# A sliding-window attention and maxout FFN kernel: its whole order of work written anew, the last outputs made ordinary units, nine buffers for first-expert results

## The chip, the cores and the metric

The kernel runs on one core of one Trainium2 chip. A core has a matrix engine (TensorE, PE in the profile; its weight loads are PEld), three engines for elementwise work (VectorE or DVE, ScalarE or ACT, GpSimd or POOL) and SyncE (SP), which here only issues DMAs. The engines run side by side, each through its own list of instructions in order, and wait for each other by semaphores. The metric is the time of one execution on the device in microseconds; lower is better.

## The reference

Two stages follow each other. First an attention over 4 batches, 8 heads, 768 positions and 64 dimensions a head, in which a query sees the 96 positions up to its own and the first 8 positions of the sequence, with a bias that falls with the distance. Then an FFN whose hidden layer is the elementwise maximum of three matrix products ("experts").

```python
scores = scale * np.matmul(q, k.transpose(0, 1, 3, 2))
is_global = pos[None, :] < 8
is_local = (rel >= 0) & (rel < 96)
keep = is_global | is_local
dist = np.where(is_global & ~is_local, 96.0, np.abs(rel))
scores = np.where(keep, scores - slopes[:, None, None] * dist, -1e9)
a = softmax(scores)
x = np.matmul(a, v)                      # 3072 tokens x 512
h = np.maximum(np.maximum(x @ w1, x @ w2), x @ w3)   # 512 -> 768
out = h @ w_out                          # 768 -> 512
```

## The kernel before

The 3072 tokens are 24 tiles T of 128, six to a batch; a pair of tiles is a group G. Tile T needs the keys and values of its own tile and of the tile before it (the first tile of a batch of its own alone, so it has half the work); the first 8 keys and values of the batch are copied into the tile's rows once the tile itself is done. The FFN takes the tiles in seven chunks of 4, 2, 2, 4, 4, 4 and 4 tiles (SIZES, line 89): chunk 0 is tiles 0 to 3, chunk 1 tiles 4 and 5, chunk 2 tiles 6 and 7, chunk 3 tiles 8 to 11, and so on to chunk 6, tiles 20 to 23.

There is no loop. The string SCHEDULE (line 24) lists some 780 units, and the last lines of the kernel call one function for each, in that order. A unit puts its instructions at the end of its engine's list, so the string fixes the order of work on every engine; the waits between engines follow from what each instruction reads and writes. A unit is a letter, its arguments with dots between, and after @ the slot of a ring of buffers that it takes. The last argument of many units is the engine: 0 is ACT, 1 DVE, 2 POOL. The units that the text speaks of:

- l (line 223): SP loads part of q, k or v of a group, 512 KB in most cases (first argument 0, 1, 2 for q, k, v; G 12 is a special first load of the first four tiles, in two halves or quarters). c casts it to bf16; v casts values into the rows of tile T.
- x (line 262): PE transposes a group's q and k, and y copies the result from PSUM; X (line 289) does both by a DMA transpose instead.
- b (line 329) puts the bias of a tile into PSUM by matmuls; S (line 338) makes the scores of four heads of tile T, 8 matmuls (4 for the first tile of a batch); e (line 352) is the exponential on ACT; m (line 359) multiplies with a mask on DVE where no bias was put in. B and K make the biases and the masks at the start. G and V copy the first 8 keys and values.
- A (line 380): weights times values, 16 matmuls (8 for the first tile of a batch); n normalises on DVE into xb. t and u transpose a tile of xb by PE and copy it into xT; Z (line 423) does it by DMA.
- w and q load the FFN's weights (staging), W and Q cast them. w123 has three column groups, w0 brings the first and w1 the two others, for expert 0, 1 or 2; q brings w_out.
- F c.f.j (line 428): the first FFN layer for chunk c, column block f of six, expert j: four matmuls of 512 columns (256 for the chunks of two tiles). f (line 441): for expert 0 the result is copied from PSUM to a buffer h01; for expert 1 DVE takes the maximum into it; for expert 2 DVE writes the maximum to ht and h01 is free.
- O c.t (line 465): the second layer for tile t of chunk c, six matmuls of 512 columns into a PSUM bank; o (line 469) copies it to a staging buffer; s (line 473) stores it. D (line 528) are matmuls on zeros into an unused bank.
- E (line 479) makes the outputs of the last chunk with its own lists of banks and buffers: tiles 0 and 1 with the sixth weight held back, tile 2, and tile 3 in parts of 256, 128 and 128 columns, each part copied and stored at once. Behind E stands one more output, `O5.0 o5.0.0 s5.0.2`, of 512 columns, stored in two halves.

PSUM has eight banks; an F or an O takes one, S and A two in a row, and the slot numbers say which. RINGS (line 90) gives the number of buffers of each ring: 7 for loads of q and k (r), 5 for h01, 3 for cast q and k (qb), 4 for transposed q and k (qkT), 4 for xb.

Of the kernel before, what the change touches and what calls it, by code (L numbers as in the profile page):

```python
# [12 lines left out]
FP32 = mybir.dt.float32  # L13
# [16 lines left out]
    w1.1@1 S0.0.0@0 e0.0@3 l2.2.2@2 S2.0.1 v0.0.1 e2.0@4 w0.1@1 v0.1.1 m0.0.1 e2.1@5 v2.1.2 b3.0@4 A1@0  # L30
    V1.1.1 V1.0.2 G2.1 v3.1.2 w0.2@2 A0@2 S3.0.1 e3.0@6 b3.1@6 n1@0 c0.2.2.2@2 S3.1.1 G3.0 A2@0 V2.0.2
    e3.1@7 V2.1.2 n0@1 t0@2 W0.0.2 c1.2.2.1 u0.0@0 x2.1.2@3 y2.1.2.0@2 w1.2@2 x2.0.2@2 A3@4 t1@6 u1.0 n2@2
    y2.0.2.1 t2@7 n3@3 l0.3.2@1 l1.3.2@2 S4.1.0@0 V3.1.2 e4.1@0 V3.0.2 S4.0.0@2 W1.1.2 u2.1 t3@6 G4.1 u3.0
    W2.0.1 S5.1.0@4 e5.1@2 S5.0.0@0 e5.0@1 m4.1.1 W1.0.1 e4.0@3 F0.5.0@7 F0.4.0@6 W2.1.0 F0.3.0@4 f0.3.0.0@0
    F0.2.0@5 f0.4.0.1@1 F0.1.0@6 v4.1.2 v4.0.2 l2.3.2@0 f0.1.0.0@2 q2@0 v5.1.0 F0.0.0@0 F0.5.1@1 F0.4.1@4
    F0.2.1@6 m4.0.1 f0.0.0.0@3 v5.0.0 f0.5.0.0@4 m5.1.1 A4@2 V4.1.0 F0.3.1@0 W0.1.2 f0.4.1.1 W0.2.0 m5.0.1
    f0.5.1.1 F0.0.1@1 F0.1.1@4 V4.0.1 W1.2.0 n4@1 t4@7 A5@2 W2.2.0 c1.3.2.2@0 f0.0.1.1 f0.1.1.1 F0.1.2@1
    n5@0 u4.1@1 f0.1.2.1@0 F0.0.2@4 q0@1 t5@7 u5.0 q1@2 f0.3.1.1 f0.0.2.1 F0.2.2@2 F0.3.2@3 f0.3.2.1
    c0.3.2.0 f0.2.0.0@2 f0.2.1.1 F1.2.0@4 F1.0.2@7 Q2.0 v7.1.2 F1.0.0@5 f1.0.0.1@3 v6.1.2 F1.0.1@3 f0.2.2.1
    f1.0.1.1 f1.2.0.1@0 Q0.2 f1.0.2.1@1 x3.1.2@6 y3.1.2.1@3 F0.4.2@5 f0.4.2.1 l1.4.2@3 v6.0.2 Q1.2 F1.1.0@0  # L40
    F1.2.2@1 l0.4.2@4 l1.6.2@5 F1.2.1@4 f1.2.1.1 F1.3.1@2 f1.2.2.1 F1.3.2@3 v7.0.2 F1.3.0@4 f1.3.0.0@2
    f1.3.1.1 f1.3.2.1 x3.0.2@1 F0.5.2@5 f0.5.2.1 F1.4.0@2 F1.1.1@3 f1.1.0.0@3 y3.0.2.0 S6.0.0@0 S6.1.0@4
    G6.2 c1.4.2.2@1 c0.4.2.2 l0.5.2@0 c0.5.2.2@2 f1.1.1.1 f1.4.0.0@1 e6.0@4 S7.0.0@6 S7.1.0@2 l1.5.2@6
    c1.5.2.2 e6.1@5 c1.6.2.2@0 e7.1@6 F1.4.1@0 e7.0@7 l2.4.2@1 O0.2@1 f1.4.1.1 m7.1.1 x4.1.2@0 F1.5.2@2
# [567 lines left out]
```

## Time and profile before

| | us |
|---|---|
| median of three runs | 176.49 |
| lowest, highest | 175.44, 176.92 |
| span of the profiled execution (first to last instruction) | 174.8 |
| PE busy | 165.9 |
| DVE busy | 131.9 |
| ACT busy | 95.4 |
| POOL busy | 54.7 |
| mean granted TensorE clock | 0.996 |

The profiled execution is one more execution, of which the page gives the span. In the rows, a line such as L433 is a line of the kernel, out<-in names what is written and read, xN counts instructions; "busy, mean ns" is followed by the idle time ahead of them and what ended it. A matmul's listed duration is longer than its pace in a queue, since queued matmuls overlap. The chain of waits names pieces of the path that ended last, with start, length and count. "SPq" rows are SP issuing a DMA; an issue grows longer when the DMA engines are behind.

### The profile page before, as it was taken

How to read it: one execution, taken by the hardware profiler on the slowest of the kernel's cores; microseconds unless marked ns; L12 is line 12 of the kernel's file. 1: busy time of each engine (PE TensorE's matmuls, PEld its weight loads, DVE VectorE, ACT ScalarE, POOL GpSimd, SP SyncE). 2: the span in 40 equal slices, each digit the busy share in tenths (PEclk: the TensorE clock that was granted, in tenths of full speed). 3: DMA queues.
4: the chain of work that ended last, by engine and by line, in shares of the span. 5: the costliest groups of instructions: out<-in, count | busy, mean ns of one | idle time of the engine just before them, and what ended most of it. 6: DMA issues, size and time to landing. Idle time of an engine off the chain costs nothing.

```text
span 174.8 us, 3865 instructions
## 1 busy us (share of the span) xinstructions
PE 165.9 (95%) x1485; PEld 93.6 (54%) x1507; DVE 131.9 (75%) x268; ACT 95.4 (55%) x147; POOL 54.7 (31%) x99
## 2 busy tenths in 40 slices
...
DMA  5999999999899899999996759998990046370035
GB/s 149 352 292 327 402 360 385 270 371 311 229 303 179 139 183 266 267 290 284 165 135 112 114 145 306 305 210 260 231 213 20 0 120 137 121 286 4 0 119 185
DMA packets 66403, 37.36 MB, mean 214 GB/s; under 512 B 24144, under 2 KB 61392, under 8 KB 66384
## 3 DMA queue, kind: packets, MB, share of 16 engines
...
q8 instruction: 12, 0.20, 0.5%
q10 hardware_dynamic: 144, 0.07, 0.1%
q14 instruction: 7, 0.06, 0.1%
...
## 4 chain that ended last, share of the span: by engine, by line
PE 76%; DVE 10%; DMA 6%; ACT 3%; issue 2%; SPq 0%; DVEq 0%
PE psum L433 44%; PE psum L457 17%; PE psum L349 6%; DMA xT<-xb 3%; DMA rawqk<-in_k_dram 3%; DVE P L365 3%; PE psum L391 3%; PE psum L394 2%; PE psum L276 2%; DVE ht L452 1%; DVE xb L403 1%; ACT P L356 1%; PE psum L270 1%; DVE qb L195 1%; PE psum L335 1%
## 5 line engine op out<-in xcount | busy, mean ns | idle before, releaser
L433 PE MATMUL psum<-xT,w 128*128 128x512 bf16 (+1 forms) x491 | 97.5, 348 | 1.5 <-DMA xT<-xb 0.7
L433 PEld LDWEIGHTS <-w 128*128 128x128 bf16 x504 | 47.6, 98 | 42.9 <-DMA xT<-xb 0.9
L356 ACT ACTIVATE P<-psum 128x1024 bf16<-128x1024 f32 (+1 forms) x48 | 43.3, 954 | 10.4 <-PE psum L349 10.3
L449 DVE TENSOR_TENSOR h<-h,psum 128x512 bf16<-128x512 bf16 (+1 forms) x42 | 25.0, 605 | 15.9 <-PE psum L433 12.4
L457 PE MATMUL psum<-wo,ht 128*128 128x512 bf16 (+2 forms) x147 | 33.4, 362 | 0.5
L447 ACT CAST h<-psum 128x512 bf16<-128x512 f32 (+1 forms) x27 | 13.8, 523 | 33.1 <-PE psum L433 29.8
L452 DVE TENSOR_TENSOR ht<-h,psum 128x512 bf16<-128x512 bf16 (+1 forms) x42 | 26.2, 644 | 2.1 <-PE psum L433 0.9
L365 DVE TENSOR_TENSOR P<-P,wmask 128x1024 bf16<-128x1024 bf16 x34 | 25.2, 752 | 2.0 <-ACT P L356 1.7
L457 PEld LDWEIGHTS <-ht 128*128 128x128 bf16 x156 | 13.8, 98 | 13.5 <-DVE ht L452 0.2
L254 POOL CAST va<-rawv 64x512 bf16<-64x512 f32 x28 | 18.5, 668 | 4.8 <-DMA rawv<-in_v_dram 3.7
L323 POOL COPY va<-vaf 4x260 int32<-4x260 int32 x17 | 7.2, 424 | 34.9 <-PE psum L394 34.5
L403 DVE TENSOR_TENSOR xb<-psum,rz 128x512 bf16<-128x512 f32 x24 | 16.6, 692 | 0.8
L201 POOL CAST qb<-rawk 128x512 bf16<-128x512 f32 x12 | 7.5, 654 | 23.7 <-DMA rawk<-in_k_dram 23.7
L349 PE MATMUL psum<-qkT 64*128 64x128 bf16 x352 | 14.4, 217 | 0.5 <-DVE qkT L315 0.4
L391 PEld LDWEIGHTS <-P 128*128 128x128 bf16 x192 | 12.6, 97 | 3.2 <-ACT P L356 0.4
L349 PEld LDWEIGHTS <-qkT 64*128 64x128 bf16 x352 | 10.0, 94 | 7.9 <-issue 5.9
L391 PE MATMUL psum<-va,P 128*128 128x65 bf16 x160 | 12.7, 193 | 0.7 <-DVE ht L452 0.6
L447 DVE CAST h<-psum 128x512 bf16<-128x512 f32 (+1 forms) x15 | 9.1, 615 | 5.1 <-PE psum L433 5.1
L471 ACT COPY staging<-psum 128x512 f32<-128x512 f32 x14 | 8.2, 592 | 8.8 <-PE psum L457 8.8
L201 POOL CAST qb<-rawq 128x512 bf16<-128x512 f32 x14 | 8.9, 664 | 9.0 <-DMA rawq<-in_q_dram 5.0
L394 PEld LDWEIGHTS <-P 128*128 128x128 bf16 x160 | 10.5, 97 | 2.1 <-issue 0.7
L394 PE MATMUL psum<-va,P 128*128 128x65 bf16 x128 | 9.9, 193 | 0.0
...
## 6 DMA issues: line engine op xcount, KB each, us to landing
rawv<-in_v_dram SPq DMA_DIRECT2D x12, 512.0 KB, 7.0
...
rawq<-in_q_dram SPq DMA_DIRECT2D x10, 512.0 KB, 7.1
rawk<-in_k_dram SPq DMA_DIRECT2D x10, 512.0 KB, 7.3
staging<-in_moe_w_dram SPq DMA_DIRECT2D x3, 1024.0 KB, 9.3
staging<-in_moe_w_dram SPq DMA_DIRECT2D x3, 512.0 KB, 8.8
staging<-in_moe_w_out_dram SPq DMA_DIRECT2D x3, 512.0 KB, 6.3
out_dram<-staging SPq DMA_DIRECT2D x5, 128.0 KB, 2.2
```

The source lines that it names most:

```text
L254: copies[how](heads(va(T))[64 * e:64 * e + 64, :, 0:D], src)
L349: nc.tensor.matmul(sp[:, hh, j2, ds], qT(T - ds, 1, hsl, jp), qT(T, 0, hsl, jp), start=not how, stop=True, skip_group_check=True)
L356: nc.scalar.activation(P[:, :, 0:n], sps[T, g].rearrange("p a b d n -> p (a b) d n")[:, :, 0:n], AF.Exp, bias=0.0, scale=scale)
L365: mul(P, P, wmask[:, g, :, 0:2])
L391: nc.tensor.matmul(o, P[:, i, 0], heads(va(T))[:, h], start=True, stop=(t == 0), skip_group_check=True)
L394: nc.tensor.matmul(o, P[:, i, 1], heads(va(T - 1))[:, h], start=False, stop=True, skip_group_check=True)
L403: nc.vector.tensor_tensor(out=x.rearrange("p (g h) d -> p g h d", g=2), in0=o4[:, :, :, 0:64], in1=rz[:, :, :, None].to_broadcast([128, 2, ...
L433: nc.tensor.matmul(ps, w123[f // 2][:, j, dm, (f % 2) * 128:(f % 2) * 128 + 128], xT[c][:, dm], start=(dm == 0), stop=(dm == 3))
L447: copies[how](h01, ps)
L449: nc.vector.tensor_max(h01s[c, f], h01s[c, f], ps)
L452: nc.vector.tensor_max(dst, h01s[c, f].rearrange("p (t e i) -> p t e i", e=2, i=64), ps.rearrange("p (t e i) -> p t e i", e=2, i=64))
L457: nc.tensor.matmul(po, ht[c][:, f, tt * 128:(tt + 1) * 128], wo[:, f, cols], start=(f == 0), stop=(f == NF - 1))
```

## The change

The string is written anew: 802 units for 782, with nearly the same work in another order and with other engines and slots for many of the casts and copies.

- Before F0.4.0, now the first F, stand S0 to S7 (before: S0 to S5 ahead of F0.5.0) and the transposes of group 3. Loads l0.2, l1.2, l1.3 and l0.3 stand ahead of the first weight load w1.0 (before: l0.2 and l1.2), and the weights come in the order w1.0, w0.1, w0.0, l2.2, w0.2, w1.1, w1.2.
- Bias units b: 4 for 7; masks m: 44 for 41. D: 10 matmuls of 512 columns and 18 of 256 in four units (before 10 and 3).
- Tiles 6 and 7 go to xT by DMA (Z) instead of PE (t, u): 17 Z for 15, 7 t for 9.
- Output copies o on DVE: 11 whole ones and one of 128 columns (before 6 and one). Value casts v on POOL: 23 for 32.
- E is gone. O, o and s take optional ranges of weights (f0 to f1) and of columns in steps of 64 (c0 to c1). The last chunk's tiles are ordinary units between the last tiles of chunk 5; tile 6.3 comes in three parts: columns 384 to 511 early, then, last of all, 0 to 255 and 256 to 383. s0.1, s0.3 and s3.3 are stored among them.
- RINGS: h01 9 for 5; r 6 for 7, qb 2 for 3, qkT 3 for 4, xb 3 for 4, rz 3 for 4.

```diff
-RINGS = {'r': 7, 'rv': 3, 'qb': 3, 'qkT': 4, 'sp': 2, 'h': 8, 'P': 8, 'xb': 4, 'xT': 3, 'wst0': 3, 'wst1': 3, 'ht': 2, 'h01': 5, 'rz': 4, 'os': 12}
+RINGS = {'r': 6, 'rv': 3, 'qb': 2, 'qkT': 3, 'sp': 2, 'h': 8, 'P': 8, 'xb': 3, 'xT': 3, 'wst0': 3, 'wst1': 3, 'ht': 2, 'h01': 9, 'rz': 3, 'os': 12}
...
+    def u_O(slot, c, tt, f0=0, f1=NF, c0=0, c1=8):
+        if slot is not None:
+            pos[c, tt, c0] = ring("h", slot, [128, (c1 - c0) * 64], FP32, "po")
+        for f in range(f0, f1):
+            nc.tensor.matmul(pos[c, tt, c0], ht[c][:, f, tt * 128:(tt + 1) * 128], wo[:, f, c0 * 64:c1 * 64],
+                             start=(f == 0), stop=(f == NF - 1))
...
+    def u_o(slot, c, tt, *rest):
+        c0, c1 = rest[:-1] or (0, 8)
+        osts[c, tt, c0] = ring("os", slot, [128, DM], FP32, "ost")[:, 0:(c1 - c0) * 64]
+        copies[rest[-1]](osts[c, tt, c0], pos[c, tt, c0])
...
+    def u_s(slot, c, tt, c0=0, c1=8, queue=0):
+        (nc.sync, nc.scalar)[queue].dma_start(out=out[T * 128:(T + 1) * 128, c0 * 64:c1 * 64], in_=osts[c, tt, c0])
```

The new order where the text speaks of it: the start up to the first F units, the start of chunk 3, and the end.

```text
l0.12.1@0 l1.12.1@1 D10.512@0 l0.12.2@2 R B2.0 B6.0 l0.12.3@3 l1.12.3@4 B4.0 B7.1 K6 c1.12.1.1@0 B0.1 K5 K7 K0
B5.0 c0.12.1.2@1 x12.0.1@0 y1.0.1.1@0 l1.12.2@5 y0.0.1.0@1 K1 K4 K3 l2.0.2@0 D2.256@1 x12.1.1@1 B3.1 y0.1.1.1
...
S6.1.0@0 e6.1@7 u2.1 u3.1 W2.0.2 F0.4.0@6 W0.1.1 F0.0.1@7 F0.1.1@4 v5.1.2 F0.1.0@5 W0.2.0 f0.1.0.0@0 V3.1.1
...
F2.0.1@2 f2.0.1.1 F2.2.0@3 f2.4.0.1@1 c0.7.2.2@1 X13@1 Z8@1 F2.3.2@7 f2.2.0.0@4 X12 l1.7.2@4 c1.7.2.2 Z10 Z9
...
o5.1.1@6 s5.1 s0.3 O6.2@4 s0.1 o6.3.6.8.0@1 s6.3.6.8 o6.2.1@2 s6.2 s3.3 O6.0.0.5.0.8@5 O6.0.5.6.0.8 o6.0.1@10
s6.0 O5.2@4 o5.2.1@6 s5.2 O6.1.0.5.0.8@5 O6.1.5.6.0.8 o6.1.1@1 s6.1 O5.0@4 o5.0.0@3 s5.0 O6.3.0.6.0.4@5
o6.3.0.4.0@10 s6.3.0.4 O6.3.0.6.4.6@6 o6.3.4.6.1@2 s6.3.4.6
```

168 lines of the change are left out of this document (61 added, 107 removed).

## The prediction

> **What bounds the kernel now.** I read the page's head and shares first, then busy time by stretch, the groups by shape, the waits of TensorE, and last the timeline of the start and the end.
>
> ```profile
> span 174.8 us, 3865 instructions
> PE 165.9 (95%) x1485; PEld 93.6 (54%) x1507; DVE 131.9 (75%) x268; ACT 95.4 (55%) x147; POOL 54.7 (31%) x99
> ...
> DMA  5999999999899899999996759998990046370035
> ```
>
> TensorE (PE) is busy for 95% of the span. The DMA line is at 9 until about 85 us, so in the first half the DMA engines are full too. The next fence cuts the span at the first and the last matmul of the first layer of the FFN and at the last matmul of all: window, its length, busy us of PE, PEld, DVE, ACT, POOL, clock, DMA share, GB/s.
>
> ```profile
> 1.19:21.58 20.39, 18.88 (x235) 11.15 (x236) 18.06 (x51) 17.50 (x31) 8.56 (x17) 1.00 1.07 321
> 21.58:171.17 149.59, 146.98 (x1250) 82.43 (x1271) 113.55 (x215) 76.90 (x116) 45.57 (x77) 1.00 0.83 203
> 171.17:174.80 3.63, 0.00 (x0) 0.00 (x0) 0.00 (x0) 0.58 (x1) 0.00 (x0) 0.81 0.43 144
> ```
>
> So the time is a sum of four terms: start 21.58 (until unit F0.5.0), PE work behind it 146.98, PE idle in that stretch 149.59 - 146.98 = 2.61, and a tail of 3.63 behind the last matmul: 174.80. A new order can't remove the work; it can win only in the other three terms, 2.61 + 3.63 and what the start wastes. The page lists no time for the profiled execution beside its span; the median of the runs is 176.49, 1.69 above it, and I carry these 1.69 over.
>
> **The change, term by term.** First the work. The rows give the pace of queued matmuls:
>
> ```profile
> 58.27 2.18 PE psum L433 x20
> 60.45 0.55 PE psum L349 x16
> 155.42 9.23 PE psum L433 x42
> 54.95 0.45 PE psum L418 x8
> ```
>
> A 512-column matmul is paced at 9.23/42 = 0.22 us, one of 256 columns (the x20) at 0.11, a score unit S (8 matmuls) at 0.275, a transpose at 0.056. Counted in the two orders: bias units b go from 7 to 4 (14 matmuls to 8: -4 x 0.22 - 2 x 0.11 = -1.1), PE transposes t from 9 to 7 (-8 x 0.056 = -0.45), warm-up matmuls D from 10 + 3 to 10 + 18 narrow ones (+15 x 0.11 = +1.65). The b and the D all lie ahead of F0, where PE waits anyway (20.39 - 18.88 = 1.5 idle, and the D are filler), so they count nothing by themselves; if they ran late they'd cost at most their 1.65. The six matmuls of the last output tile are still 512 columns in all (before 256 + 128 + 128, after 128 + 256 + 128), and splitting the sums of two other tiles at 5 of 6 weights adds none. Ahead of F0 the new order also does S6 and S7 (2 x 0.14 + 2 x 0.275 = 0.83; tile 6 has one block) and the transposes x3 (16 x 0.056 = 0.90). Work behind F0: 146.98 - 0.83 - 0.90 - 0.45 (t6, t7) = **144.8**.
>
> **The start** is where the new order pays. Here are the exponentials, the first weight's cast and the loads:
>
> ```profile
> 6.34 2.65 SPq L236 DMA_DIRECT2D rawq<-in_q_dram  x1
> 9.11 1.90 SPq L236 DMA_DIRECT2D rawk<-in_k_dram  x1
> 11.05 3.52 SPq L514 DMA_DIRECT2D staging<-in_moe_w_dram  x3
> ...
> 9.06 1.02 ACT L356 ACTIVATE P<-psum 128x1024 bf16<-128x1024 f32 x1 [0.30 <-PE psum L349]
> 11.32 3.54 ACT L356 ACTIVATE P<-psum 128x1024 bf16<-128x1024 f32 x4
> 21.75 1.67 POOL L201 CAST w<-staging 128x512 bf16<-128x512 f32 x2 [3.20 <-DMA staging<-in_moe_w_dram]
> ...
> L201 POOL CAST qb<-rawq 128x512 bf16<-128x512 f32 x14 | 8.9, 664 | 9.0 <-DMA rawq<-in_q_dram 5.0 <-DVE va L325 4.0
> L195 DVE CAST qbq<-rawqq 128x1024 bf16<-128x1024 f32 x1 | 0.7, 694 | 0.1
> ...
> staging<-in_moe_w_dram SPq DMA_DIRECT2D x3, 1024.0 KB, 9.3
> staging<-in_moe_w_dram SPq DMA_DIRECT2D x3, 512.0 KB, 8.8
> ...
> DMA to landing us min/median/max: 7.9/9.2/11.3
> ```
>
> F0.4.0 needs the weight w1.0. Before, four loads of 512 KB stood between the quarter loads and it; now six do (l1.3.2, l0.3.2 moved ahead). At the stretch's 321 GB/s two loads of 0.524 MB are 3.3 us, so w1.0 is issued near 11.05 + 3.3 = 14.3 and lands 9.3 later, at 23.6. Its cast W2.0 moves from DVE to POOL, where a pair of halves takes 1.67 by the row above (1.2 is the best pair): F0 at 24.8 to 25.3. The other chain is ACT: from e1.1 to e6.0, which frees the banks for S6.1 just ahead of F0, it has ten wide exponentials at about 0.95 (three of the 3.54 above and the short one), three short ones at 0.55, and 2.6 of copies: 13.75. From 9.06 that ends at 22.8; the first query cast also moves to POOL (0.66 a half against 0.69 for the whole on DVE) and K1, K4, K3 go ahead of y1.1.1, so e1.1 is rather at 9.6: 23.4, and t3, u3 behind n3 bring it to about 24.3. I take **24.8**: the weight is the later chain. Bounds: 14.3 + 7.9 + 1.2 = 23.4 and 14.3 + 11.3 + 1.7 = 27.3. The following weights (w0.1, w0.0, w0.2, w1.1, w1.2) come at 1.6 us per 512 KB, each about as PE wants it (0.88 per F unit, eight units until w0.2), so they have no cover left; I count 0.2.
>
> **Idle behind F0.** Three waits of before:
>
> ```profile
> PEld L433 <- DMA xT<-xb: 0.9, 1, 0.9
> PE psum L433 <- DMA xT<-xb: 0.7, 1, 0.7
> PE psum L391 <- DVE ht L452: 0.6, 1, 0.6
> ...
> 110.80:111.58 0.78, 0.61 (x16) 0.43 (x14) 0.25 (x1) 0.00 (x0) 0.00 (x0) 1.00 1.15 315
> ...
> L447 ACT CAST h<-psum 128x256 bf16<-128x256 f32 x8 | 2.9, 375 | 5.0 <-PE psum L433 5.0
> L195 ACT CAST qb<-rawq 128x1024 bf16<-128x1024 f32 x2 | 2.1, 1046 | 0.1
> ...
> L424 SPq DMA_TRANSPOSE xT<-xb x15: 1188/1487/2670, 63.0 to 145.2; - x15
> DMA to landing us min/median/max: 2.4/3.4/7.0
> ```
>
> The 0.7 is chunk 3 waiting for its DMA-transposed tiles at 72.8; the 0.6 is A12 waiting for DVE at 83.1; A13 at 111 costs 0.78 - 0.61 = 0.17. The rest of 2.61 (1.2) is spread thin; I keep it. Chunk 3 again: X13 goes out only behind c1.6.2.0 on ACT (0.38 for f2.3.0, 0.22 and 0.59 for the small copy and the output copy between, 1.05 for the cast: 2.2 after F2.3.0), then Z8, X12, l1.7.2, Z10 and Z9 leave SP one after another (four at 1.49, one load 0.58), so Z9 starts 8.8 after F2.3.0 and lands 3.4 later, at 12.2. PE's work in that stretch, summed as above (14 F units of two tiles, two A, one t, three O at 1.3, five S), is 12.4. Wait 0 to 1.4; I take 0.4. Chunk 2 now comes by Z6, Z7 instead of t6, t7: they lie behind X10, which needs c0.5.2.0 behind e8.1; landing about 11 us after S8 against 11.5 of PE work: 0.2. Chunks 4, 5, 6 have 7.1, 5.5 and 5.3 us of PE work between the last A and the first F against about 1.6 of normalising plus 3.4: nothing, though 5.0 of landing would cost 1. Idle: 1.2 + 0.2 + 0.4 + 0.2 = **2.0**, between 1.2 and 4.
>
> DVE carries more, POOL less:
>
> ```profile
> L365 DVE TENSOR_TENSOR P<-P,wmask 128x1024 bf16<-128x1024 bf16 x34 | 25.2, 752 | 2.0 <-ACT P L356 1.7
> L471 DVE COPY staging<-psum 128x512 f32<-128x512 f32 x6 | 4.1, 684 | 0.2 <-PE psum L457 0.2
> L283 DVE COPY qkT<-psum 128x512 bf16<-128x512 bf16 x4 | 2.6, 685 | 0.0
> L254 POOL CAST va<-rawv 64x512 bf16<-64x512 f32 x28 | 18.5, 668 | 4.8 <-DMA rawv<-in_v_dram 3.7
> ```
>
> Three more masks (2.3), five more output copies (3.4), four more y copies (2.7), with the smaller moves +7 us, to 139; POOL loses nine value casts (-6). PE's 165 still covers DVE. The nine h01 buffers let first-expert results leave PSUM early and cost nothing; the smaller rings (r, qb, qkT, xb, rz one less each) delay loads, the tightest being X20, still about 2 us ahead of S20.
>
> **The tail.**
>
> ```profile
> 171.19 0.58 ACT L471 COPY staging<-psum 128x512 f32<-128x512 f32 x1 [1.03 <-PE psum L457]
> 171.80 0.81 SPq L477 DMA_DIRECT2D out_dram<-staging  x2
> ...
> L462 DVE COPY staging<-psum 128x128 f32<-128x128 f32 x1 | 0.3, 291 | 3.1 <-PE psum L457 3.1
> L462 ACT COPY staging<-psum 128x256 f32<-128x256 f32 x1 | 0.4, 372 | 0.1
> ...
> out_dram<-staging SPq DMA_DIRECT2D x5, 128.0 KB, 2.2
> out_dram<-staging SPq DMA_DIRECT2D x1, 64.0 KB, 2.1
> ```
>
> Before: copy 0.58, second issue near 172.2, landing 2.2, 0.4 to the end. After: the 256-column copy ends 0.06 after the last matmul, its issue takes 0.41, then the last 64 KB go: 0.48 + 2.1 + 0.4 = **3.0**, 0.6 less. It would be 3.6 if the outputs saved up for the end (s0.1, s0.3, s3.3) fill the queue.
> [...]
>
> **Sum:** 24.8 + 144.8 + 2.0 + 3.0 = 174.6, against 174.8; with 1.69, **176.3 us**, no change. The start gives away 3.2 and has 1.7 of it back as work done early; t, idle and tail bring 0.45, 0.6 and 0.6.
>
> **Rivals.** *The weights come early and the new order's slack is real.* Start 23.4, idle 1.2: 23.4 + 144.8 + 1.2 + 3.0 = 172.4, time 174.1. For it: before, DVE's cast of w1.0 found it there without a listed wait. Against: POOL waited 3.2 us for w0.0.
> *The weights come late* (the other side): w1.0 at the row's 11.3, start 27.3, and each weight behind it late as well, idle 3.2: 27.3 + 144.8 + 3.2 + 3.0 = 178.3, time 180.0. It decides once the start passes 27, or 26 with over 2.8 of idle.
> *DVE becomes the bound* between F0 and F1, where, counted unit by unit with the rows' durations, it has 11.8 against 11.1 on PE: +0.7 there and as much at chunk 2, 176.0, time 177.7. Against: a worse ratio before chunk 3 of the old order (16.4 on 14.5, counted alike) cost 0.7.
> *It doesn't do what it says:* the tail stays 3.6: 175.2, time 176.9.
> *The array goes cold while it waits for weights.* The first ten matmuls pace 0.43 instead of 0.22:
>
> ```profile
> 1.19 4.45 PE L532 MATMUL psum<-zeros 128*128 128x512 bf16 x10 [1.19 <-DVE cap L550]
> ```
>
> If PE idles long enough ahead of F0, eight F units at that pace cost 8 x 4 x 0.21 = 6.7 more, time 183.0; the widest gap by the bounds is 27.3 - 24.3 = 3.0.
> [...]
>
> **How the numbers follow.** Forecast 0.40, early weights 0.31, late weights 0.19, DVE 0.06, tail 0.03, cold 0.01. About 1% is what a measurement of this kernel tells from no change: faster is under 174.7, slower over 178.3. Faster 0.31, within 1% 0.49, slower 0.20. The range reaches from a little below the early case to short of the late one, 173.4 to 179.2; the forecast's own is 174.8 to 178.2.
>
> **What would show it.** First L433 matmul near 24.8 with a wait of PE or POOL on the weight's DMA; PE busy behind it near 144.8; a wait on xT near F3 under 1.4 and none by DVE at A12 and A13; the last matmul to the end 3.0. The prediction is wrong if F0 starts before 23.4 or after 27.3, or if idle behind F0 exceeds 4.

## The result, and the profile after

The changed kernel takes **184.15 us** (median; 182.88 to 185.23) against 176.27 for the kernel before beside it (175.44 to 176.92): a ratio of 1.0449, interval 1.0388 to 1.0510. The forecast was 176.3, with a range up to 179.2. The change is slower, by 7.9 us. The profile below is of the longest of its four executions, 185.23 us.

The head of the page after, with the shares of PE and the DMA line:

```profile
span 183.5 us, 3876 instructions
PE 168.8 (92%) x1487; PEld 94.9 (52%) x1508; DVE 138.1 (75%) x274; ACT 96.5 (53%) x149; POOL 50.9 (28%) x91
PEclk9999969999999999999999999999999999999999
DMA  4999999999917899999998999998903870030294
```

Two things are new: a 6 in the line of the granted clock, in the slice from 22.9 to 27.5 us, and a 1 in the DMA line, in the slice from 50.5 to 55 us, where the line of before has 9. Now the same three stretches as in the prediction: until the first F, from there to the last matmul, and the tail.

```profile
1.19:28.17 26.98, 22.46 (x285) 14.37 (x286) 19.98 (x53) 21.08 (x35) 15.66 (x27) 0.94 1.08 306
28.17:179.31 151.14, 146.37 (x1203) 80.54 (x1224) 117.51 (x218) 74.88 (x115) 34.69 (x59) 1.00 0.79 191
179.31:183.50 4.19, 0.00 (x0) 0.00 (x0) 0.29 (x1) 0.07 (x1) 0.00 (x0) 0.91 0.38 129
```

| term, us | before | forecast | after | after less forecast |
|---|---|---|---|---|
| start | 21.58 | 24.8 | 28.17 | +3.4 |
| PE busy behind F0 | 146.98 | 144.8 | 146.37 | +1.6 |
| idle behind F0 | 2.61 | 2.0 | 4.77 | +2.8 |
| tail | 3.63 | 3.0 | 4.19 | +1.2 |
| sum | 174.8 | 174.6 | 183.5 | +8.9 |

All four terms miss to the same side. The sum misses by 8.9 and the median by 7.9, since this execution lies 1.1 above the median. Busy and idle have to be read together, as 1487 of 1508 matmul records are there, and 1485 of 1507 in the profile before. Together they are 151.14 against 146.8, +4.3. Two runs of experiment 10 kept every record. On the kernel before with the new tail, the stretch of 148.90 holds 148.27 busy and 0.63 idle. In the kernel after with three stores moved, which changes nothing in PE's list, the stretch is:

```profile
28.01:179.88 151.87, 147.82 (x1227) 80.57 (x1224) 117.74 (x218) 74.84 (x115) 34.68 (x59) 1.00 0.78 190
```

That is 4.05 idle. So most of the 2.61 of idle before was records that are missing, and the change adds about 3.4 us of idle behind F0.

**The start.** The timeline of PE and of POOL there (it lists the first F from 28.10 on):

```profile
21.09 0.19 PE L384 MATMUL psum<-va,P 128*128 128x65 bf16 x1 [1.60 <-POOL va L247]
26.84 0.73 PE L342 MATMUL psum<-qkT 64*128 64x128 bf16 x20 [0.34 <-DVE qkT L280]
28.10 1.25 PE L426 MATMUL psum<-xT,w 128*128 128x512 bf16 x4
...
14.71 1.92 POOL L194 CAST qb<-rawk 128x512 bf16<-128x512 f32 x2
16.58 1.17 POOL L194 CAST qb<-rawq 128x512 bf16<-128x512 f32 x2
18.30 2.74 POOL L247 CAST va<-rawv 64x512 bf16<-64x512 f32 x2
24.73 1.17 POOL L194 CAST w<-staging 128x512 bf16<-128x512 f32 x2
```

A2 stands 1.60 us for the values of tile 2. Their cast v2.1.2 is the second of the pair at 18.30, behind v3.1.2 and the casts c1.2 and c0.2. The weight that the forecast called the late chain is cast from 24.73 to 25.9, and the first F comes 2.2 later. In between, the clock falls. The trace records half clock from 22.30 to 25.72; these are that stretch and the 3.41 us ahead of it:

```profile
18.89:22.30 3.41, 1.69 (x39) 1.46 (x39) 2.17 (x6) 2.12 (x5) 2.31 (x4) 1.00 1.07 361
22.30:25.72 3.42, 3.42 (x47) 2.74 (x45) 2.69 (x5) 2.31 (x3) 3.30 (x6) 0.50 1.10 347
```

**Chunk 3.** SP stands at X10 from 46.2 to 54.24, and behind X10 on SP stand Z6, Z7 and all later loads and transposes. The totals of waits, a window of the time in which SP stands, and PE from F3 on:

```profile
SPq L285 <- ACT qb L188: 7.0, 2, 3.6
...
PEld L426 <- DMA xT<-xb: 1.4, 1, 1.4
...
52.00:54.00 2.00, 2.00 (x20) 1.25 (x19) 1.27 (x3) 2.00 (x3) 1.31 (x3) 1.00 0.01 4
...
79.01 5.34 PE L426 MATMUL psum<-xT,w 128*128 128x512 bf16 x23 [0.98 <-DMA xT<-xb]
84.87 0.19 PE L387 MATMUL psum<-vaf,P 128*128 128x65 bf16 x1 [0.48 <-POOL vaf L247]
92.92 0.20 PE L384 MATMUL psum<-va,P 128*128 128x65 bf16 x1 [0.60 <-DVE P L358]
95.18 4.48 PE L426 MATMUL psum<-xT,w 128*128 128x512 bf16 x19 [0.49 <-DVE ht L445]
```

Almost no transfer runs from 52 to 54 (share 0.01). The two waits of X on ACT, 7.0 together, are X10's for c0.5.2.0 (3.4) and X13's for c1.6.2.0 (3.6). Ahead of its 3.4, X10 stands for another 4.6 us for PE: it takes over the buffer of tiles 6 and 7, which the scores S8 still read. In that time the loads issued earlier still fill the DMA engines (share 1.09 from 48 to 50). The ring has a third buffer, which nothing uses until X18; no run gave it to X10. F3 starts at 79.0, against 72.8 before, and has idled 0.98 for its transposed tiles; the weight load's 1.4 for them runs at the same time. In the expectations below the two are added up as 2.4, which counts one wait twice. Behind F3 PE waits for A13's values, for A12's mask and for DVE again. By parts, F0 to F3, F3 to F4, and F4 to the last matmul:

```profile
28.17:79.01 50.84, 49.41 (x483) 32.22 (x492) 42.24 (x88) 35.16 (x53) 14.75 (x26) 1.00 0.94 235
79.01:109.03 30.02, 27.98 (x242) 14.12 (x247) 23.15 (x42) 16.75 (x27) 10.91 (x18) 1.00 0.98 193
109.03:179.31 70.28, 68.98 (x479) 34.20 (x488) 52.12 (x90) 22.97 (x35) 9.03 (x16) 1.00 0.60 157
```

PE idles 1.43, 2.04 and 1.30 us in them; with every record, in the run with the stores moved, it is 1.05, 2.39 and 0.60.

**The tail.** The last issues, the last copy, and the sizes with their landing times:

```profile
178.96 1.30 SPq L463 DMA_DIRECT2D out_dram<-staging  x3
179.34 0.29 DVE L459 COPY staging<-psum 128x128 f32<-128x128 f32 x1 [1.59 <-PE psum L453]
...
out_dram<-staging SPq DMA_DIRECT2D x2, 64.0 KB, 2.6
out_dram<-staging SPq DMA_DIRECT2D x1, 128.0 KB, 3.0
```

The copy is as short as forecast (0.29). But the last issue ends 0.95 behind the last matmul, and the landing is 2.6 to 3.0 instead of 2.1.

### The profile page after: what moved, and what is told of

It reads as the page before. It is cut to its first block, busy times and chain, and to the rows that moved or that the text cites. A ratio compares the mean times of both kernels' runs of the same rounds, so it can differ in the third digit from the quotient of the medians.

```text
span 183.5 us, 3876 instructions
## 1 busy us (share of the span) xinstructions
PE 168.8 (92%) x1487; PEld 94.9 (52%) x1508; DVE 138.1 (75%) x274; ACT 96.5 (53%) x149; POOL 50.9 (28%) x91
## 4 chain that ended last, share of the span: by engine, by line
PE 64%; DVE 11%; issue 3%; ACT 3%; DMA 3%; POOL 1%; SPq 1%; POOLq 0%; DVEq 0%; ACTq 0%
PE psum L426 38%; PE psum L453 15%; PE psum L342 4%; DVE P L358 3%; DMA rawv<-in_v_dram 3%; PE psum L384 3%; PE psum L387 2%; DVE h L442 2%; DVE ht L445 2%; ACT P L349 2%; PE psum L269 1%; DVE xb L396 1%; SPq L417 1%; DVE va L247 1%; POOL vaf L247 1%
## 5 line engine op out<-in xcount | busy, mean ns | idle before, releaser
L426 PE MATMUL psum<-xT,w 128*128 128x512 bf16 (+1 forms) x490 | 98.3, 348 | 2.4 <-DMA xT<-xb 1.0
L426 PEld LDWEIGHTS <-w 128*128 128x128 bf16 x504 | 47.4, 98 | 43.4 <-DMA xT<-xb 1.4
L358 DVE TENSOR_TENSOR P<-P,wmask 128x1024 bf16<-128x1024 bf16 x36 | 27.8, 794 | 3.2 <-ACT P L349 2.9
L442 DVE TENSOR_TENSOR h<-h,psum 128x512 bf16<-128x512 bf16 (+1 forms) x42 | 24.6, 603 | 7.1 <-PE psum L426 6.8
L445 DVE TENSOR_TENSOR ht<-h,psum 128x512 bf16<-128x512 bf16 (+1 forms) x42 | 25.2, 641 | 1.2 <-PE psum L426 0.5
L459 ACT COPY staging<-psum 128x512 f32<-128x512 f32 (+2 forms) x14 | 7.5, 550 | 30.9 <-PE psum L453 21.0
L247 POOL CAST va<-rawv 64x512 bf16<-64x512 f32 x16 | 12.8, 799 | 19.3 <-DMA rawv<-in_v_dram 18.5
L194 POOL CAST qb<-rawk 128x512 bf16<-128x512 f32 x14 | 10.4, 768 | 26.0 <-DMA rawk<-in_k_dram 25.8
L384 PE MATMUL psum<-va,P 128*128 128x65 bf16 x160 | 13.2, 196 | 2.4 <-POOL va L247 1.6
L395 DVE RECIPROCAL rz<-psum 128x8 f32<-128x8 f32 x24 | 4.8, 201 | 10.9 <-PE psum L387 10.8
L316 POOL COPY va<-vaf 4x260 int32<-4x260 int32 x14 | 5.9, 423 | 22.7 <-PE psum L387 18.3
L459 DVE COPY staging<-psum 128x512 f32<-128x512 f32 (+1 forms) x12 | 7.8, 653 | 5.4 <-PE psum L453 5.0
```

Source lines behind the costliest of these rows:

```text
L247: copies[how](heads(va(T))[64 * e:64 * e + 64, :, 0:D], src)
L358: mul(P, P, wmask[:, g, :, 0:2])
L384: nc.tensor.matmul(o, P[:, i, 0], heads(va(T))[:, h], start=True, stop=(t == 0), skip_group_check=True)
L426: nc.tensor.matmul(ps, w123[f // 2][:, j, dm, (f % 2) * 128:(f % 2) * 128 + 128], xT[c][:, dm], start=(dm == 0), stop=(dm == 3))
L442: nc.vector.tensor_max(h01s[c, f], h01s[c, f], ps)
L445: nc.vector.tensor_max(dst, h01s[c, f].rearrange("p (t e i) -> p t e i", e=2, i=64), ps.rearrange("p (t e i) -> p t e i", e=2, i=64))
```

## The experiments

Each run names its edit to the order; where nothing else is said it is an edit to the kernel after. In the new kernels the lines stand three lower (L426 of the page after is L429). Times are medians; in brackets the ratio to the kernel before with its interval. "F0", "F3" and "last" are the starts of the first F of chunks 0 and 3 and the end of the last matmul, in the profiled execution.

| run | us | ratio | F0 | F3 | last | span |
|---|---|---|---|---|---|---|
| after | 184.15 | 1.0449 | 28.1 | 79.0 | 179.3 | 183.5 |
| v2.1.2 first | 183.34 | 1.0415 | 26.0 | 78.3 | 178.1 | 182.3 |
| filler in the wait | 184.56 | 1.0487 | 27.0 | 77.7 | 179.2 | 182.5 |
| c1.6 forward | 187.85 | 1.0694 | 27.9 | 83.0 | 182.8 | 187.3 |
| stores forward | 184.77 | 1.0478 | 28.0 | 79.0 | 179.9 | 183.9 |
| l1.6 forward | 185.32 | 1.0555 | 27.0 | 78.3 | 178.5 | 183.1 |
| l1.6 and c1.6 forward | 184.87 | 1.0514 | 27.1 | 79.1 | 179.2 | 183.5 |
| and l2.6, v2.1.2 | 184.76 | 1.0506 | 25.7 | 78.7 | 179.1 | 183.3 |
| c0.5 forward | 184.01 | 1.0424 | 27.2 | 77.4 | 178.1 | 182.5 |
| all five | 183.05 | 1.0373 | 26.0 | 77.2 | 177.0 | 181.3 |
| and casts off POOL | 182.64 | 1.0391 | 26.2 | 77.6 | 176.0 | 180.2 |
| and no fillers | 180.53 | 1.0265 | 26.4 | 76.7 | 175.3 | 178.5 |
| casts off POOL, stores forward | 181.59 | 1.0295 | 26.2 | 77.5 | 176.6 | 180.1 |
| all of these | 180.26 | 1.0257 | 26.2 | 76.7 | 175.6 | 178.8 |
| no fillers alone | 183.97 | 1.0470 | 27.2 | 78.7 | 178.7 | 181.8 |
| weights first, tiles 6, 7 later | 193.86 | 1.1018 | 25.3 | 90.8 | 189.1 | 193.6 |
| weights first | 189.95 | 1.0793 | 32.2 | 82.6 | 182.6 | 186.9 |
| before, new tail | 175.85 | 0.9983 | 21.5 | 72.0 | 170.4 | 174.0 |
| before, new tail, no D3 | 175.64 | 0.9992 | 21.7 | 72.1 | 170.2 | 173.8 |

**1. The value cast** (the order on POOL alone).

```diff
-l2.3.2@0 c1.3.2.1@0 v3.1.2 v2.1.2 A2@6
+l2.3.2@0 c1.3.2.1@0 v2.1.2 v3.1.2 A2@6
```

> The cast of the values of tile 2 (v2.1.2) stands ahead of that of tile 3 (v3.1.2) on POOL; nothing else is moved. Value-cast theory (A2 waits for POOL, the wait of 1.6 us is followed by half clock): v2.1.2 ends 1.37 us sooner, A2's wait falls from 1.60 to about 0.2 us, the granted clock stays over 0.8 between 20 and 26, and the first F0 starts 1.5 to 3 us sooner than 28.17, so 181 to 183 us. Late-weight theory (w1.0 behind two loads): F0 unchanged at 28.2, 184 us. Theory of the exponentials' chain (ACT alone sets F0): F0 at most 0.5 us sooner, 183.7.

Measured: 183.34 us (1.0415, 1.0381 to 1.0449). The timeline:

```profile
12.19 0.61 POOL L250 CAST va<-rawv 64x512 bf16<-64x512 f32 x1
...
18.20 2.14 POOL L250 CAST va<-rawv 64x512 bf16<-64x512 f32 x2
24.59 1.18 POOL L197 CAST w<-staging 128x512 bf16<-128x512 f32 x2 [1.05 <-DMA staging<-in_moe_w_dram]
...
25.82 0.29 PE L345 MATMUL psum<-qkT 64*128 64x128 bf16 x4 [0.30 <-ACT P L352]
26.04 3.20 PE L429 MATMUL psum<-xT,w 128*128 128x512 bf16 x13
```

A2 no longer waits, the clock stays at 1, and F0 comes 2.06 sooner. So the swapped pair of casts did set F0. Now POOL waits 1.05 for the weight (landed at 24.59; forecast 23.6), its cast ends at 25.77, and the exponential of tile 6 releases PE at 25.82: the two chains of the forecast, under 0.1 apart. But the end comes only 1.2 sooner in the profile and 0.8 in the median, where the intervals overlap, and misses the 181 to 183 expected: F3 is only 0.7 sooner, so most of what the start gains is given back before it.

**2. The clock alone.** Twelve filler matmuls inside the wait; A2 starts no sooner.

```diff
-S4.0.0@2 e4.0@3 l1.4.2@1
+S4.0.0@2 e4.0@3 D12.256@0 l1.4.2@1
```

> 12 matmuls of 256 columns on the constant tile (as the kernel's own D units, results not used) stand ahead of A2, nothing is moved. Cold-clock theory (the wait of 1.6 us itself costs little, the half clock behind it costs the rest): PE idles some 0.3 us instead of 1.6 there, the granted clock between 22 and 26 stays near 1 instead of 0.58, and F0 starts 1 to 1.7 us sooner than 28.17 though A2 starts no sooner; 182.3 to 183 us. Theory that the wait alone counts: F0 unchanged or up to 1 us later, 184 to 185. Late-weight theory: 184.

Measured: 184.56 us (1.0487, 1.0440 to 1.0534). The profile has the clock at 1 and F0 at 27.0, 1.1 sooner, as expected; the median doesn't move. Six more runs leave the start up to F0 as it is after, or only lack fillers, and they split by themselves. With half clock (c1.6 forward, stores forward, and after): F0 at 27.9, 28.0, 28.1. Without (l1.6 forward, l1.6 and c1.6, c0.5 forward, fillers left out): 27.0, 27.1, 27.2, 27.2, though PE waits the same 1.60 or 1.61 for POOL. So half clock costs F0 0.9 us in such an execution, and the wait for the cast another 1.1. The times agree: of the kernel after, the executions with a mean granted clock of 0.989 and 0.986 took 185.23 and 184.86, those with 0.997 and 1.000 took 183.43 and 182.88; with l1.6 forward it was 186.11 and 185.73 at 0.985 and 0.984, and 184.92 and 184.79 at 1.000. The four executions with the filler in the wait, all at 0.997 or more, took 183.30 to 185.09; why they are not as short as the others at that clock stays open. What decides between the two isn't shown. With c0.5 forward, where the clock stays at 1, these are the 3.41 us in which the same wait begins and the 3.42 in which it ends:

```profile
16.89:20.30 3.41, 2.44 (x39) 1.93 (x34) 3.38 (x7) 3.36 (x6) 3.29 (x6) 1.00 1.16 310
20.30:23.72 3.42, 2.67 (x64) 2.25 (x65) 2.13 (x5) 2.05 (x3) 2.25 (x6) 1.00 1.06 371
```

**3. The weights first**, the step on which the forecast rested.

```diff
-l1.3.2@3 l0.3.2@4 w1.0@0 w0.1@0 w0.0@1
+w1.0@0 w0.1@0 w0.0@1 l1.3.2@3 l0.3.2@4
```

> The kernel after with the loads l1.3.2 and l0.3.2 behind w1.0, w0.1 and w0.0 on SP instead of ahead of them; nothing else is moved. This is the step on which the forecast rested (w1.0 behind two loads sets the first F0). Weight theory: w1.0 lands 3 us sooner, F0 starts 2 to 3 us sooner than 28.1, 181 to 182.5 us. Value-cast and cold-clock theory: the weights are not what is late, F0 stays within 0.5 us of 28.1 or comes later by the later x3; 184 to 186 us.

Measured: 189.95 us (1.0793, 1.0726 to 1.0861), F0 at 32.2. The weight theory is wrong in sign, and the 184 to 186 of the other is missed too. The weight does go sooner: w1.0 is issued at 11.16 instead of 14.93. DVE and PE at the place of the wait:

```profile
25.44 0.70 DVE L191 CAST qb<-rawk 128x1024 bf16<-128x1024 f32 x1 [5.64 <-DMA rawk<-in_k_dram]
...
26.19 1.03 PE L272 MATMUL psum<-identb,qb 128*128 128x128 bf16 x8 [4.89 <-DVE qb L191]
```

The new order has c1.3.2.1 on DVE, and S6 and S7 on PE, ahead of F0. Without the keys of tiles 6 and 7 DVE stands, and everything behind it. The two loads ahead of w1.0 aren't a price of the new order; they are what its start needs.

**4. Tiles 6 and 7 behind F0**, with the weights first, on top of the edits of 7 and 8 below. The units that the lines put in are taken out where they stood, in lines left out here.

```diff
-l1.3.2@3 l0.3.2@4 w1.0@0 w0.1@0 w0.0@1
+w1.0@0 w0.1@0 w0.0@1 l1.3.2@3 l0.3.2@4
...
-F0.1.0@5 W0.2.0
+F0.1.0@5 c1.3.2.1@0 c0.3.2.2 x3.1.2@3 y3.1.2.1@0 W0.2.0
...
-u5.0 F1.4.0@0
+u5.0 S6.0.0@0 e6.0@1 S7.1.0@3 e7.1@2 S7.0.0@0 e7.0@6 S6.1.0@3 e6.1@7 m6.0.1 m7.0.1 m6.1.1 F1.4.0@0
```

> On top of the run with the casts off POOL: w1.0, w0.1, w0.0 ahead of l1.3.2 and l0.3.2 on SP; the casts c1.3, c0.3 and the transposes x3 behind the first units of F0 (x3 in bank 3), the scores and exponentials of tiles 6 and 7 behind u5.0 (in banks 0, 1 and 3, 4), with their masks. Theory that tiles 6 and 7 ahead of F0 set the start: F0 starts at 22.5 to 24 instead of 26.2 although the weights alone first made it 32.2; 2.0 us of PE's work go behind F0, and about 1 us of wait for the exponentials, so 180.5 to 182.5 us. Theory that weights or values set it: F0 later than 25.5, 183 to 185.

In this order the scores of tile 7 go into bank 3 while sums of F0.3.0 still stand there, so those sums are overwritten; the time is read as a time. Measured: 193.86 us. F0 is at 25.3, behind waits of 1.12 and 0.85 for DVE's normalising and its copy of xT, and half clock follows at once (0.50 from 26 to 28, 0.65 from 28 to 30). Behind F0 a weight's cast on DVE stands behind the copies of x3, PE waits 1.51 for it, and the clock falls again, to 7 and 5 tenths in the page's slices from 33.9 to 43.6. The wait only moved, and neither theory's time came. The run doesn't tell what sets the last 4 us of the start.

**5. The cast for X13.**

```diff
-v10.0.0 v10.1.0 f2.3.0.0@8 G10.0 V9.1.2 V9.0.2 A10@4 o1.1.0@11 c1.6.2.0
+c1.6.2.0 v10.0.0 v10.1.0 f2.3.0.0@8 G10.0 V9.1.2 V9.0.2 A10@4 o1.1.0@11
```

> The cast c1.6.2.0 on ACT stands ahead of v10.0.0 and v10.1.0, 7 units earlier; nothing else is moved. Theory that SP's wait for this cast (3.6 us) holds X13 and behind it Z9 and the load l2.6.2: SP's wait falls under 1 us, X13, Z9 and l2.6.2 go 2 to 3 us sooner, the waits of F3 for xT (2.4 us) fall under 0.5 and A13's for its values (0.5) goes: 181.5 to 182.5 us. Theory that DVE is the bound of chunk 3 (75 per cent busy, masks at 794 ns): the waits for xT become waits for DVE, within 0.7 us of the kernel after, 183.5 to 184.5.

Measured: 187.85 us (1.0694, 1.0650 to 1.0738), 3.7 slower than after. ACT and PE:

```profile
67.39 1.04 ACT L191 CAST qb<-rawk 128x1024 bf16<-128x1024 f32 x1 [3.63 <-DMA rawk<-in_k_dram]
...
69.65 0.22 PE L387 MATMUL psum<-va,P 128*128 128x65 bf16 x1 [4.07 <-ACT va L250]
```

Both theories failed: ACT met a load that hadn't landed, the value casts behind it stood too, and behind PE's wait of 4.07 the clock fell (0.85 on average from 70 to 80). The keys l1.6.2 are what is late for a cast at that place. So the load was moved, alone and with the cast:

```diff
-X10@0 l2.5.2@0 Z6@2 Z7 F0.3.1@0 F1.3.2@3 F1.3.1@2 f1.3.1.1 X11
+X10@0 l1.6.2@3 l2.5.2@0 Z6@2 Z7 F0.3.1@0 F1.3.2@3 F1.3.1@2 f1.3.1.1 X11
...
-F1.1.2@0 l1.6.2@3 f1.1.2.1
+F1.1.2@0 f1.1.2.1
```

> The load of the keys of tiles 12 and 13 (l1.6.2) goes right behind X10 on SP, ahead of l2.5.2, Z6, Z7 and X11; nothing else is moved. Late-load theory (in the run before, the cast c1.6.2.0 moved forward stopped ACT for 3.63 us because this load had not landed; so the load, not the cast, holds X13): the load is issued near 54 instead of 60.8, ACT waits no more for it, X13 goes at 65.5 to 66 instead of 67.25, the wait ahead of S12 and F3 falls by 1 to 1.5 us: 182.5 to 183.3 us. Cast theory (the place of c1.6.2.0 on ACT alone holds X13): X13 within 0.3 us of 67.25, 184.

> The load l1.6.2 early as in the run with that alone, and the cast c1.6.2.0 ahead of v10.0.0 on ACT as in the run that was slower by 2 per cent. Late-load theory: ACT's wait of 3.63 us goes, X13 goes at 63 to 65 instead of 67.25, F3 waits under 1 us for xT instead of 2.4: 181.3 to 182.8 us. If the 187.9 us of the cast alone came from its place on ACT and not from the load, it stays over 186.

Measured: 185.32 (1.0504 to 1.0605) and 184.87 (1.0471 to 1.0557). The pair of edits takes back 3.0 of the 3.7 us, so the load was the cause of that; but neither run is better than after, and the gains that the late-load theory expected are not there. Then l2.6.2 went ahead of X13 and v2.1.2 ahead of v3.1.2 as well:

> Both edits of the run before, and the load of the values of tiles 12 and 13 (l2.6.2) ahead of X13 on SP, and v2.1.2 ahead of v3.1.2 on POOL. If start and chunk 3 are the two places of the loss: F0 starts at 26.0 as with v2.1.2 alone, and the 2 us are kept this time (with v2.1.2 alone they were given back ahead of S12), A13 waits for no value: 178.5 to 181 us. If DVE is the bound of chunk 3: 181.5 to 183, with over 9.7 of 10 us of DVE somewhere between 75 and 105.

Measured: 184.76 (1.0467 to 1.0544); F0 at 25.7, F3 at 78.7, so 2.4 us of the start gave F3 0.3, and the time lies above both ranges. SP in front of chunk 3:

```profile
62.17 2.05 SPq L232 DMA_DIRECT2D rawv<-in_v_dram  x2
64.39 5.08 SPq L288 DMA_TRANSPOSE qkT<-qb  x1
```

X13's issue starts 2.9 us sooner than in the kernel after (64.39 against 67.25), but it takes 5.08 us instead of 2.21, behind two value loads, and so ends at the same time.

**6. The wait that empties the queue.** X10's cast goes ahead of the cast Q2.0 on ACT.

```diff
-Q2.0 S8.0.0@4 e8.0@1 V7.0.0 e8.1@7 c0.5.2.0 X10@0
+c0.5.2.0 Q2.0 S8.0.0@4 e8.0@1 V7.0.0 e8.1@7 X10@0
```

> The cast c0.5.2.0 goes ahead of Q2.0 on ACT, 8 units forward; nothing else is moved. Idle-transfer theory (in the kernel after, SP stands at X10 from 46.2 to 54.24 for this cast, no transfer runs from 52 to 54 (share 0.01), and all later loads and transposes, which fill the queues to 76, come late by it): X10 goes at 50.9 (behind S8, whose tile it takes over) instead of 54.24, the last transpose of chunk 3 at 70 to 71.5 instead of 73.4, the waits of F3 fall from 2.4 to under 0.8 us: 181 to 182.5 us. Late-load theory of the runs before: already without effect there, 184. Theory that DVE bounds chunk 3 whatever the transfers do: 183.5 to 184.5, DVE over 9.8 of 10 us between 90 and 100.

Measured: 184.01 us (1.0424, 1.0359 to 1.0488). The empty stretch is gone:

```profile
52.00:54.00 2.00, 2.00 (x27) 1.27 (x26) 1.90 (x4) 0.98 (x2) 0.75 (x2) 1.00 1.16 125
```

X10 goes at 50.28 instead of 54.24 and F3 at 77.4 instead of 79.0, but the median stays: the idle-transfer theory's 181 to 182.5 us is wrong, and 184 is what the two others had. DVE is busy for 9.83 of the 10 us from 90 on, as the DVE theory has it.

**7. All five together** (v2.1.2, l1.6.2, l2.6.2, c1.6.2.0, c0.5.2.0).

> The three edits that together gave 184.8 (l1.6.2 and l2.6.2 forward, c1.6.2.0 forward, v2.1.2 first) and c0.5.2.0 ahead of Q2.0. Idle-transfer theory: SP is held up no more, so the other edits now count: F0 at 26, the last transpose of chunk 3 at 68 to 70.5: 177.5 to 180.5 us. Theory that DVE bounds chunk 3: 182 to 184.5.

Measured: 183.05 us (1.0373, 1.0332 to 1.0414): 1.1 better than after with intervals that overlap, short of the 177.5 to 180.5 expected, and inside the DVE theory's range. F3 is at 77.2 and waits for transposes no more; now PE waits for DVE between 88 and 94. DVE and POOL there:

```profile
89.38 3.01 DVE L361 TENSOR_TENSOR P<-P,wmask 128x1024 bf16<-128x1024 bf16 x3
...
88.97 1.86 POOL L197 CAST qb<-rawq 128x512 bf16<-128x512 f32 x2
91.14 1.73 POOL L197 CAST qb<-rawk 128x512 bf16<-128x512 f32 x2 [0.31 <-DMA rawk<-in_k_dram]
```

Three masks take 3.01, and the POOL casts 1.7 to 1.9 instead of the 1.17 of the pairs at 16.58 and 24.73 in the profile after.

**8. The casts off POOL**, on top of 7.

```diff
-c0.8.2.2@1 S12.1.0@4
+S12.1.0@4
...
-c1.8.2.2 S15.1.0@2
+S15.1.0@2
...
-V13.0.0 X16@1 F3.4.2@6
+V13.0.0 F3.4.2@6
...
-m15.1.1 f3.0.1.1
+m15.1.1 c0.8.2.0@1 c1.8.2.0 X16@1 f3.0.1.1
```

> On top of the run with all four fixes: the casts c0.8 and c1.8 go from POOL to ACT, behind e15.1, and X16 behind them; nothing else is moved. Contention theory (in that run POOL's casts at 88.97 to 92.8 and DVE's masks and value casts, 1.00 us instead of 0.67 and 0.84 instead of 0.43 at the same time, slow each other, and PE waits 1.95 us for DVE at 88.5, 91.4 and 93.7): the masks between 88 and 93 take 0.70, the three waits sum to under 0.9 us, 181.3 to 182.2 us. Load theory (DVE has too many instructions there, whoever runs beside it): waits 1.6 to 2 us, 182.8 to 183.3.

Measured: 182.64 us (1.0391, 1.0326 to 1.0456); the profile:

```profile
89.46 1.90 DVE L361 TENSOR_TENSOR P<-P,wmask 128x1024 bf16<-128x1024 bf16 x3
...
84.00:88.00 4.00, 3.99 (x49) 2.01 (x48) 3.88 (x8) 3.45 (x6) 1.75 (x3) 1.00 1.20 290
88.00:92.00 4.00, 3.43 (x31) 1.61 (x29) 3.94 (x8) 3.81 (x5) 0.95 (x3) 1.00 1.47 171
92.00:96.00 4.00, 3.93 (x26) 1.94 (x25) 3.93 (x9) 1.49 (x3) 0.31 (x1) 1.00 0.61 107
96.00:100.00 4.00, 4.00 (x44) 2.19 (x42) 3.73 (x7) 2.10 (x5) 0.00 (x0) 1.00 0.76 179
```

The same three masks take 1.90, so POOL's casts did slow them. The waits at A12 and behind it are gone (one of 0.57 at 89.0 is left), F3 to F4 shrinks from 29.7 to 28.3 us, and the span is 1.1 shorter. In the median the gain of 0.4 isn't told from none: the contention theory has the profile right, and its 181.3 to 182.2 us wrong.

**9. The fillers**, left out on top of 8, and then alone from the kernel after.

```diff
-l2.0.2@0 D2.256@1 x12.1.1@1
+l2.0.2@0 x12.1.1@1
...
-D5.256@0 S1.1.1
+S1.1.1
...
-D6.256@2 S0.0.0@2
+S0.0.0@2
...
-D5.256@0 S4.0.0@2
+S4.0.0@2
```

> On top of the run with the casts off POOL: the four groups of filler matmuls D2.256, D5.256 (twice) and D6.256 of the new start are left out (18 matmuls of 256 columns on the constant tile, no part of the result); D10.512 stays. Filler theory: they lie on the path to F0, which starts 1 to 2 us sooner than 26.2; 180.5 to 181.7 us. Cover theory (they fill waits, and hold the clock): F0 at 26.0 to 26.5 and 182.4 to 183, or, if the granted clock falls below 0.9 in some stretch before 26, later by up to 1.5 us and 183 to 184.5.

> The kernel after without D2.256, D5.256 (twice) and D6.256 (18 matmuls of 256 columns on the constant tile, no part of the result); nothing else is changed. If fillers cost by themselves (they stand in front of scores that wait for nothing else): 182 to 182.6 us, 1.6 to 2.1 under the kernel after, whatever its clock does. If they only fill waits: 183.8 to 184.5. If they hold the clock (which the change put them there to do, by their place ahead of waits): 185 to 186, with more stretches of half clock before 28.

Measured: 180.53 us (1.0265, 1.0211 to 1.0319) on top of 8, and 183.97 (1.0429 to 1.0511) alone. On top of 8, with all its matmul records, the stretch from F0 to the last matmul and the tail are:

```profile
26.39:175.30 148.91, 146.70 (x1227) 80.64 (x1224) 116.78 (x218) 76.84 (x117) 29.76 (x55) 1.00 0.81 197
175.30:178.50 3.20, 0.00 (x1) 0.00 (x0) 0.29 (x1) 0.08 (x1) 0.00 (x0) 1.00 0.47 161
```

Alone, leaving the fillers out changes nothing that is measured, as if they only fill waits. On top of 8 it gave 2.1 us, though F0 comes at 26.4 as with them, and the clock even fell once, to 0.50 from 11.9 to 15.3; in that profile 1.1 is gained between F0 and F3, and 1.0 in the tail. The time is in the filler theory's range, but the sooner F0 that it rests on is not there. Why the fillers matter only there stays open.

**10. The tail.** The late stores forward, from after and from 8:

```diff
-o5.1.1@6 s5.1 s0.3 O6.2@4 s0.1
+o5.1.1@6 s5.1 O6.2@4
...
-s4.2 f6.0.2.1@0
+s4.2 s0.3 s0.1 s3.3 f6.0.2.1@0
...
-s6.2 s3.3
+s6.2
```

> The stores s0.3, s0.1 and s3.3, put off to the last units by the change, go right behind s4.2; nothing else is moved. Theory that they crowd the last transfers: last matmul to end falls from 4.19 to 3.2 us, 183.1 to 183.3 us. Rival, that the small last transfer's own landing sets the tail: 4.0 to 4.3, 184.1.

> On top of the run with the casts off POOL: s0.3, s0.1 and s3.3 behind s4.2 instead of among the last units. Late-store theory: last matmul to end 3.6 instead of 4.2 us, 182.0 us. Landing theory (as with the same edit on the kernel after alone, 4.0 against 4.19): 4.0 to 4.3, 182.4 to 182.9.

Measured: 184.77 us, tail 4.0 (1.0403 to 1.0554), and 181.59, tail 3.5 (1.0295, 1.0234 to 1.0355). The first is no gain. The second is 1.05 under its base, but the intervals overlap, and in the profiles its tail is 0.7 shorter and its last matmul 0.55 later, so a gain isn't shown. Then the ordinary units and the part of 128 columns on the kernel before, with its own order and rings:

```diff
-s5.3.2
+s5.3
...
-E@7 O5.0@2 o5.0.0@5 s5.0.2
+O6.0.0.5.0.8@6 O6.1.0.5.0.8@7 O6.0.5.6.0.8 o6.0.0@8 s6.0 O6.1.5.6.0.8 o6.1.0@2 s6.1 O6.2@3 o6.2.0@0 s6.2
+O6.3.0.6.0.4@0 o6.3.0.4.0@10 s6.3.0.4 O6.3.0.6.6.8@1 o6.3.6.8.1@11 s6.3.6.8 O5.0@2 o5.0.0@5 s5.0
+O6.3.0.6.4.6@4 o6.3.4.6.1@7 s6.3.4.6
```

> The kernel before with its own order and buffer counts, but the last unit E and what follows it written as ordinary units, a part of 128 columns of the last tile at the end, as the change has it. My forecast of this part: tail 3.0 instead of 3.63, 0.6 us faster, 175.5. Rival, that the landing of the last transfer sets the tail whatever its size (the kernel after: 4.19, with the late stores moved away 4.0): 176 to 176.6. Work of PE is the same to 0.1 us.

Measured: 175.85 us (0.9983, 0.9956 to 1.0011). The stretches from F0 and behind the last matmul:

```profile
21.46:170.36 148.90, 148.27 (x1272) 82.60 (x1271) 114.16 (x215) 76.89 (x116) 45.62 (x77) 1.00 0.82 204
170.36:174.00 3.64, 0.01 (x1) 0.00 (x0) 0.29 (x1) 0.34 (x1) 0.00 (x0) 1.00 0.35 122
```

It is 3.64 against 3.63: the new form of the tail is worth nothing. With these units the tail was 3.1 to 4.5 over the runs: it scatters by more than the form changes.

**11. A version to beat both.** Everything that helped on top of after, and the kernel before with the new tail and without D3.256:

> All edits to the kernel after together: v2.1.2 first, l1.6.2 and l2.6.2 forward, c1.6.2.0 and c0.5.2.0 forward, c0.8 and c1.8 on ACT, the stores s0.3, s0.1, s3.3 behind s4.2, the fillers out. If the effects add: 179.4 to 180.0 us (180.5 without the stores, whose edit took 1.0 there). If the store effect is the scatter of the last landing: 180.3 to 181. Slower than the kernel before in either case: 144.2 us of PE's work stand behind F0 before and 142.2 after, but F0 starts 4.5 later.

> The kernel before with the ordinary tail (as in the run of the tail on the kernel before, 175.85) and without D3.256 (three matmuls of the constant tile at 6.4, no part of the result). If a filler costs its own time on PE there (0.33 us): 175.4 to 175.6. If it lies in a wait: 175.85. If the clock falls without it: 177 to 178.5.

Measured: 180.26 us (1.0257, 1.0237 to 1.0277) and 175.64 (0.9992, 0.9968 to 1.0016). The first is about what the run without the stores' edit gave (180.53), so the 1.05 of that edit doesn't add; the second doesn't tell a cost of D3.256 from none. Nothing tried is faster than the kernel before beyond its measurement. In the best version of the new order F0 comes at 26.2 and F3 at 76.7; with the old order 21.5 and 72.0. So all that is left, 4.4 us in the median, is there by F0 and carried to the end; which chain of the start sets it stays open. The 2.2 us that the forecast took off PE's work behind F0 don't come back as time.

## Why the prediction was wrong, step by step

**The step that failed** is "I take 24.8: the weight is the later chain". The start came at 28.1, and idle behind F0 at 4.77: both are signs that the forecast itself had named for being wrong. No rival foretold 184; the nearest were the late weights (180.0) and the cold array (183.0). Experiment 1 shows 2.1 us of the difference in the start: the cast of tile 2's values waits on POOL behind that of tile 3, and, in this execution, half clock follows. The forecast had counted POOL's casts as work moved and not looked at their place in POOL's queue. POOL was at 15.66 of 26.98 us there, against 8.56 of 20.39 before. The other 1.2 are sizes in the forecast's two chains: with the values first, the weight landed at 24.6, not 23.6, and the exponentials' chain ended at 25.8, not 24.3. The two loads do put the weight off, by 3.8 us at its issue (experiment 3), but with them behind w1.0 the start is 4 us worse, as S6 and S7 need them.

**The cold array**, given a chance of 0.01, is the rival that happened in part. It reckoned with one gap of at most 3.0 us, for weights; behind a gap of 1.60, for values, the clock fell to 0.50. Its price was 0.9 us at F0 and not 6.7, as the clock came back after 3.42 us. The forecast had no measured number for how long PE has to idle before the clock falls. Its own row of the tail before shows a fall, with a mean clock of 0.81. Cut where the trace records the fall, it is:

```profile
170.02:173.44 3.42, 1.14 (x6) 0.29 (x3) 0.00 (x0) 0.73 (x2) 0.00 (x0) 1.00 0.78 278
173.44:174.83 1.39, 0.00 (x0) 0.00 (x0) 0.00 (x0) 0.00 (x0) 0.00 (x0) 0.50 0.06 20
```

The clock fell 2.3 us behind the last matmul, and PE had worked for 1.14 of the 3.42 us ahead of that. So the profile before already showed a fall behind a gap shorter than the 3.0 us of the forecast.

**Idle behind F0.** It was 4.77 instead of 2.0. "Wait 0 to 1.4; I take 0.4" for chunk 3 came out at 0.98, inside its bounds, but by luck: both sums that it is the difference of were too small. From F2.3.0 (64.25) to F3 PE is busy for 13.6 us instead of 12.4. X13 goes 3.0 after F2.3.0 instead of 2.2, its issue takes 2.21 and those of Z10 and Z9 3.71, where the forecast has 1.49 for each, and Z9 lands near 79.0, 14.7 after F2.3.0 instead of 12.2. The forecast had also left out X10, which stood for c0.5.2.0 while no transfer ran (experiment 6). Freeing it shows that this one wait doesn't carry the loss: F3 comes 1.6 sooner, the end 1.0 in the profile, and the median doesn't move. The larger idle is between F3 and F4 (2.04): A12 and A13, which the forecast had without a wait, wait 0.60 and 0.48.

**"PE's 165 still covers DVE"** was wrong where it mattered. DVE's sum came out as forecast (+6.2 against +7), but from 84 to 100 us DVE is busy for 15.5 of 16 us in the run of experiment 8, and slowed by POOL in that of 7. It isn't shown how much of the time this costs. A sum over the span says nothing about sixteen microseconds of it. The forecast had checked DVE at F0 to F1 and at chunk 2, and not at chunk 3.

**The work**: the forecast took 2.2 off, 1.7 for work done ahead of F0 and 0.45 for transposes moved to DMA. In runs with every matmul record PE is busy behind F0 for 146.70 (no fillers) to 147.82 (stores forward), where the kernel before with the new tail has 148.27: -0.5 to -1.6 of the -2.2, though the new order has the same 1227 matmuls there in each. In the profile after, records that are missing blur the term.

**The tail**: "0.6 less" failed twice. The form gives nothing (3.64 against 3.63), and in the profile after the tail was longer: the last issue ended 0.95 behind the last matmul instead of 0.48, and the two pieces of 64 KB took 2.6 to land instead of 2.1.

**What held**: chunk 2 (no wait on its transposes in the profile after); DVE's added work; the fillers, which "count nothing by themselves" (0.2 us alone, not told from none).
